# Block 0's rows written and asked for three units earlier, and three more x tiles made by ScalarE and GpSimd

## The chip, the cores and the metric

One core of one Trainium2 chip runs the whole kernel in a single launch. The metric is the device time of an execution in microseconds (us). TensorE is written PE here (PEld is its weight load), VectorE DVE, ScalarE ACT, GpSimd POOL, SyncE SP; SP issues nearly all DMA, POOL the indirect ones.

## The reference, cut to what matters

A decayed linear attention over 768 steps for 4 batches and 8 heads of 48, whose output rows (3072 of 384 numbers) go through a mixture of 8 experts, one expert for each row:

```python
for t in range(S):
    cur = np.einsum('bhd,bhe->bhde', u[None] * kt, vt)
    y[:, :, t] = np.einsum('bhd,bhde->bhe', rt, state + cur)
    state = wt[:, :, :, None] * state + np.einsum('bhd,bhe->bhde', kt, vt)
x = y.transpose(0, 2, 1, 3).reshape(B * S, H * D)
logits = x @ w_gate + modality_bias[modality_id]
e_idx = np.argmax(logits, axis=1)
for e in range(E):
    h = np.maximum(x[mask] @ w1[e], 0.0)
    out[mask] = gate_w[mask, None] * (h @ w2[e])
```

With the inputs drawn, 2663 rows go to expert 1 and 409 to expert 6. Of the rows of expert 1, the first five units of 128 rows hold 544 and the first ten 1110.

## The kernel before, in words

**Attention.** The 3072 rows are 24 units of 128 rows, six for each batch. A software pipeline runs `att_iter(i)` for i from -2 to 23. In iteration i it decays and scales the inputs of unit a = i + 2 (DVE makes the two scans B and E and then R; POOL makes K and G), multiplies keys with queries for unit m = i + 1 (PE; DVE masks the result to A; ACT carries the state) and makes the output of unit z = i on PE in the PSUM bank pY. One iteration later `x_rows(z - 1)` adds the term dV, which POOL makes, to pY and stores the row tile x (tile xp). It does so in one of two ways: DVE adds both in one instruction, or, for the iterations in `BY_TWO`, ACT copies pY to xp and POOL adds dV in place. One iteration after that, `x_cols` transposes x on PE and `logits` multiplies it with the gate.

PSUM is short: pK holds R's input of the next unit until DVE has made R, and PE's transposes of K into pK come after that; pY is written by the next unit's products only when x has read it.

**Routing.** At the end of iterations 11 and 12 two hooks route the first group of units (`CUT`: units 0 to 9): the row's expert, and by counting products on PE (`route_b`) the row's place `posT` in the DRAM table xs, which holds 3584 rows for each expert. A queue `pend` then holds the ten units; `drain(n)` takes n of them and lets POOL write their x rows to xs with an indirect DMA each (`scatter`). The other 14 units are routed and written while the experts run.

**Experts.** Rows are worked on in blocks of 512. Block 0 always takes the first 512 rows of expert e0, which is known from the biases alone. `blk_load(0)` reads them from xs with one DMA on SP's queue (tile xl) and one of the gate values (xg); `blk_t(0)` transposes xl on PE; then `blk_up` and `blk_down` run for each of eight slices of the hidden layer, each product three times with the weights split into a high part wh and a low part wl. The weights are split by ACT (wh) and POOL or DVE (wl), those of block 0 in iterations 22 and 23 (`w_splits`) and after. `table(0)` tells what block 1 is: it needs `hd`, which is 1 for e0 if block 0 was full.

**What sets the order.** Every engine has one queue in program order, written out by hand. `pend`, `hooks` and the sets `BY_TWO` and `SPLITS` set what goes into which iteration. SP waits at its head instruction, POOL too.

In the profile's lines, L241 is K, L306 G, L302 dV, L238 R, L347 A, L424 x by DVE, L421 and L422 x by ACT and POOL, L639 the scatter, L320 the transposes of K, L434 those of x, L272, L372, L384 and L387 further products of an iteration, L662 the load of xl, L687 its transposes, L709 and L731 the experts' products, L230 a half slice of wl.

Of the kernel before, what the change touches and what calls it, by code (L numbers as in the profile page):

```python
# [14 lines left out]
ALU = mybir.AluOpType  # L15
# [3 lines left out]
P = 128  # L19
NCH = S // P  # L20
NU = B * NCH
NT = B * S
DM = H * D
E, F = 8, 1024
# [5 lines left out]
BT = 512  # L30
# [20 lines left out]
NG = 8  # L51
CUT = (0, 10, NU)
NJS = (CUT[1], NU - CUT[1])
GW = B * H * S * D // (P * NG)
WHALF = FC // 2 * DM

# [2 lines left out]
def kernel(ctx: ExitStack, tc: tile.TileContext, rkw, vt, wf, cst, mid, wg, bias, w1, w2, out):  # L59
# [24 lines left out]
    T = {}  # L84

    def wt(n, tag, sh, bufs=None, dt=F32):
        T[tag, n] = (pa if tag in PREP else wk if tag in WORK else rt).tile(sh, dt, tag=tag, name=f"{tag}{n}", bufs=bufs)
        return T[tag, n]
# [68 lines left out]
    onesb = cp.tile([P, P], BF16, name="onesb")  # L157
# [13 lines left out]
    oh0 = cp.tile([P, E], F32, name="oh0")  # L171
# [68 lines left out]
    def mk_k(a, k):  # L240
        nc.gpsimd.tensor_tensor(out=wt(a, "K", [P, 4, P]), in0=quarters(k), in1=quarters(T["B", a][:, 1:517])[:, :, 1:129], op=ALU.mult)  # L241
# [23 lines left out]
    def ok(n):  # L265
        return 0 <= n < NU

    def delta(m, pT):
        G = T["G", m]
        for p in range(4):  # L270
            for q in (0, 64):
                nc.tensor.matmul(out=pT[q:q + 64, DM + 2 * p:DM + 2 * p + 2], lhsT=G[:, p * P + q:p * P + q + 64], rhs=ub[:, p, 0:2],  # L272
                                 start=True, stop=True, skip_group_check=True)
        nc.scalar.copy(out=wt(m, "dT", [P, 4, 2], 3), in_=pT[:, DM:DM + 8].rearrange("p (a b) -> p a b", a=4))

    st = quarters(pt("st", "pU")[:, 0:4 * D])
    hooks = []
    done = iter(range(2 * FC))

    SPLITS = {NU - 2: 4, NU - 1: 8}  # L280
    BY_TWO = (1, 4, 7, 8, 9, 10, 11)

    def w_splits(i):
        for _ in range(SPLITS.get(i, 0)):
# [2 lines left out]
    def att_iter(i):  # L287
        a, m, z = i + 2, i + 1, i
# [14 lines left out]
                                    in1=T["dT", z].rearrange("p a b -> p (a b)")[:, :, None].to_broadcast([P, H, D]), op=ALU.mult)  # L303
        if ok(a):
            mk_k(a, k)
            nc.gpsimd.tensor_tensor(out=wt(a, "G", [P, 512]), in0=r, in1=k, op=ALU.mult)  # L306
        if i == NU - 1:
            w_splits(i)
        if ok(z - 1):
            x_rows(z - 1, i in BY_TWO)  # L310
        last = first(m + 1)
        if ok(m):
            K, R, v = T["K", m], T["R", m], T["v", m]
# [36 lines left out]
            mk_r(a)  # L350
        if ok(m):
            delta(m, pT)
            if i < NU - 1:
                w_splits(i)
            if not last:
                for h in range(H):
                    p, hh = divmod(h, 2)

                    nc.tensor.matmul(out=st[64 * hh:64 * hh + rows, p], lhsT=KT[:, h],
                                     rhs=v[:, h * D:(h + 1) * D], start=first(m) and p == 0, stop=True, skip_group_check=True)  # L360
                carry(m)
# [92 lines left out]
    def rcol(o, *sh):  # L454
        n = 1
        for d in sh:
            n *= d
        v = T["R"][:, o:o + n]
        return v if len(sh) == 1 else v.rearrange("p (a b) -> p a b", a=sh[0])

    C_RK = NU * E
# [31 lines left out]
    def route_b(c):  # L493

        oh, nj = T["oh", c], NJS[c]
        sh, NE = [P, nj, E], nj * E
        pR = T["R"][:, C_RK:C_RK + NE + E]

        def add(out, lhsT, rhs, start=False, stop=False):
            nc.tensor.matmul(out=out, lhsT=lhsT, rhs=rhs, start=start, stop=stop, skip_group_check=True)  # L500

        add(pR[:, 0:NE], trib, oh.rearrange("p a b -> p (a b)"), c == 1)
        add(pR[:, 0:NE], onesb, ersb[:, None, :].to_broadcast(sh))
        if c:
            add(pR, onesb, ohs[:, None, :].to_broadcast([P, nj + 1, E]))

        for j in range(nj):
            add(pR[:, (j + 1) * E:], onesb, oh[:, j:j + 1].to_broadcast([P, nj - j, E]), stop=j == nj - 1)
        po, rk = posT[:, CUT[c]:CUT[c + 1]], rcol(C_RK, nj, E)
        nc.vector.tensor_tensor(out=rk, in0=rk, in1=oh, op=ALU.mult)  # L510
        with nc.allow_low_precision("whole numbers"):
            nc.vector.tensor_reduce(out=po, in_=rk, axis=AX.X, op=ALU.add)
# [3 lines left out]
    def table(ph):  # L516
# [51 lines left out]
        if ph == 0:  # L568
            rounded(g, ct, 1.0 / BT, -0.5 + 0.5 / BT)
            hd = wt(ph, "hd", [P, E], 1)  # L570
            tt(out=hd, in0=g, in1=oh0, op=ALU.min)
            tt(out=g, in0=g, in1=hd, op=ALU.subtract)
            sums(cu, g)
            yield

            ts(out=fs, in0=cu, scalar1=float(NA - 1), scalar2=None, op0=ALU.min)
            vec.scalar_tensor_tensor(out=fA, in0=cu[:, 1:E + 1], scalar=float(NA - 1), in1=fs[:, 0:E], op0=ALU.min, op1=ALU.subtract)
            yield from rows(1, NA - 1, cu, fA, hd)
            tt(out=fA, in0=fA, in1=hd, op=ALU.add)
            return  # L580
# [222 lines left out]
    pend = []  # L803
# [3 lines left out]
    def drain(n, after=None, h=None):  # L807
        for _ in range(n):
            if pend:
                if after:  # L810
                    after(h[0:1, 0:1].bitcast(F32))
                scatter(pend.pop(0))
# [11 lines left out]
    for i in range(-2, NU):  # L824
        if 2 <= i < 7:
            hooks.append((setup_a, setup_b, setup_c, setup_d, setup_e)[i - 2])
        if i == CUT[1] + 1:
            ra, tb = route_a(0), table(0)
            hooks.extend([lambda: list(ra), lambda: hook_b(0)])
        if i == CUT[1] + 2:  # L830
            route_x(0)
        if i >= NU - 2:
            hooks.append(lambda: next(tb))
        if i == NU - 1:
            prep.close()
        att_iter(i)
        if i == NU - 1:
            for n in done:
                w_split_half(n)
        if i != -1 and ok(i + 3):  # L840
            loadv(max(i + 3, 2))
        if ok(i + 6):
            load(i + 6, ((1024, 1541),))
        if i == 4:
            e0 = nc.sync.value_load(e0i[0:1, 0:1], min_val=0, max_val=E - 1)
        for n in range(2 * FC):
            if i == (n + 4 if n < FC // 2 else NU - 10 + n if n < FC else NU - 6 + (n - FC) // 2):
                w_raw(e0, n // FC, n % FC, parts=FC)
        if ok(i + 6):
            load(i + 6, ((0, 1024),))  # L850
        if i == -1:
            clear((ersb, 0.0), (onesb, 1.0), (one8, 1.0), (mfx, 0.0), (rbx, 0.0))
        if i == 0:
            clear((zt, 0.0), (zt[:, DM:DM + 1], 1.0), (zt[:, DM + 1:DM + 2].bitcast(I32), PAD_ID), (glo, W_LO), (ghi, -W_HI))
            early()
        if i == 4:
            r0 = nc.sync.value_load(e0r[0:1, 0:1], min_val=0, max_val=(E - 1) * RS)
        if 8 <= i < 8 + JT:
            rows_apart("xz", nc.sync.dma_start(out=xs[ds(r0 + (i - 8) * P, P), :], in_=zt))

        drain(1)
        if i == NU - 3:
            assert not pend
            blk_load(0)
    assert not pend and not hooks

# [302 lines left out]
```

## Time and profile before

| | |
|---|---|
| median of 3 runs | 336.15 us (335.85 to 338.52) |
| the profiled execution | 336.19 us, of it 334.4 us from the first to the last instruction |
| TensorE's granted clock | 0.996 of full speed over the span |
| busy shares of the span | PE 96%, PEld 88%, DVE 64%, ACT 61%, POOL 59% |
| instruction queues (kind "instruction") | 33 packets on q8, 25 on q14 |
| the chain that ended last | nearly empty: the last output write of POOL, 0.98 us |

Times within the span count from its first instruction. A row of the timeline gives the start, the duration, the engine, the line and in brackets how long the engine sat idle ahead of it and what ended that; "issue" stands where no other engine or DMA in the profile explains it. Ends of PE's products are modelled, so a long row of them overlaps the next row; their starts are the better measure.

### The profile page before, as it was taken

The page shows a single profiled execution, that of the slowest core. Times are in us where ns is not written, and L with a number is a line of the kernel's source. Part 1 is how long each engine was busy: PE and PEld are TensorE (multiplying, and loading weights), DVE is VectorE, ACT ScalarE, POOL GpSimd, SP SyncE. Part 2 cuts the span into 40 slices and gives each one's busy share as a digit, 9 for nine tenths or more (in the row PEclk, how much of TensorE's full clock was granted, in tenths as well). Part 3 has the DMA queues.
Part 4 walks back from the last instruction along what each step waited for, and adds up shares of the span by engine and source line. Part 5 has one row for each costly group of instructions (what it writes and reads, how often), then busy time and mean ns, then how long its engine had stood idle before and what let it go on. Part 6 is the DMA issues. An engine that isn't in the chain of part 4 may idle for free. (4 is left out here: it accounts for less than half of the span.)

```text
span 334.4 us, 10126 instructions
## 1 busy us (share of the span) xinstructions
PE 321.6 (96%) x3942; PEld 293.1 (88%) x3943; DVE 214.4 (64%) x376; ACT 204.2 (61%) x467; POOL 196.6 (59%) x226
## 2 busy tenths in 40 slices
PE   6899998999999999999999999999999999999993
PEld 3689898988899988899889988998899889999993
DVE  6999997999999757795333965934560464054230
ACT  3887897787488775542521767656745855632150
POOL 7988987879999795676361680247024603450041
PEclk9999999999999999999999999999999999999998
DMA  7997888878998532426337037026544763360011
GB/s 273 406 347 245 294 280 241 285 243 240 301 309 263 163 97 97 95 95 215 143 119 213 0 84 250 0 73 169 185 167 165 214 233 97 95 212 5 0 74 32
DMA packets 35586, 58.66 MB, mean 175 GB/s; under 512 B 17297, under 2 KB 22089, under 8 KB 35528
## 3 DMA queue, kind: packets, MB, share of 16 engines
q1 hardware_dynamic: 32424, 48.45, 46.4%
q0 software_dynamic: 3104, 9.47, 7.6%
q8 instruction: 33, 0.54, 0.7%
q14 instruction: 25, 0.20, 0.2%
HBM read 57.86 MB, written 12.67 MB: 211 GB/s over the span
## 5 line engine op out<-in xcount | busy, mean ns | idle before, releaser
L224 POOL TENSOR_TENSOR wl<-raw,wh 128x768 fp32r<-128x768 f32 x20 | 39.0, 1954 | 73.8 <-ACT wh L223 73.7
L223 ACT CAST wh<-raw 128x768 fp32r<-128x768 f32 x48 | 39.3, 831 | 37.4 <-PE pU_d L731 23.3
L720 DVE SCALAR_TENSOR_TENSOR h<-pS_u,h 128x512 fp32r<-128x512 f32 (+2 forms) x39 | 23.2, 607 | 36.5 <-ACT h L718 36.3
L751 POOL DMA_INDIRECT out<-ot,xg x24 | 25.2, 1052 | 29.4 <-ACT ot L760 23.4
L224 DVE TENSOR_TENSOR wl<-raw,wh 128x768 fp32r<-128x768 f32 x28 | 31.0, 1113 | 14.8 <-ACT wh L223 14.4
L709 PE MATMUL pS_u<-xh,wh 128*128 128x512 f32 (+1 forms) x102 | 39.6, 388 | 0.0
L709 PE MATMUL pS_u<-xh,wl 128*128 128x512 f32 (+1 forms) x102 | 39.2, 385 | 0.0
L709 PE MATMUL pS_u<-xo,wh 128*128 128x512 f32 (+1 forms) x102 | 39.2, 384 | 0.0
L718 ACT ACTIVATE h<-pS_u 128x512 fp32r<-128x512 f32 (+1 forms) x34 | 19.8, 586 | 27.7 <-PE pS_u L709 25.4
L731 PE MATMUL pX_d<-wh,h 128*128 128x384 f32 x96 | 32.4, 337 | 0.0
L731 PE MATMUL pY_d<-wh,h 128*128 128x384 f32 x96 | 32.2, 335 | 0.0
L731 PE MATMUL pK_d<-wh,h 128*128 128x384 f32 x96 | 32.1, 334 | 0.0
L639 POOL DMA_INDIRECT xs<-xp,posT x24 | 26.1, 1088 | 9.3 <-issue 7.4
L306 POOL TENSOR_TENSOR G<-in 128x512 f32<-128x512 f32 x24 | 30.7, 1278 | 0.0
L241 POOL TENSOR_TENSOR K<-in,B 128x512 f32<-128x512 f32 x24 | 28.4, 1185 | 3.7 <-PE pY L387 1.7
L295 DVE TENSOR_TENSOR_SCAN B<-in,pX_d 128x516 f32<-128x516 f32 x24 | 29.3, 1219 | 1.8 <-DMA in<-rkw 1.8
L298 DVE TENSOR_TENSOR_SCAN E<-in,pX_d 128x516 f32<-128x516 f32 x24 | 29.5, 1229 | 0.8
L731 PE MATMUL pU_d<-wh,h 128*128 128x384 f32 x80 | 26.8, 334 | 0.0
L720 DVE SCALAR_TENSOR_TENSOR h<-pT_u,h 128x512 fp32r<-128x512 f32 (+2 forms) x17 | 9.6, 577 | 24.6 <-ACT h L718 24.6
L387 PE MATMUL pY<-v,A 128*64 128x48 f32 x368 | 25.3, 222 | 0.0
L347 DVE TENSOR_TENSOR A<-pS,m 128x768 f32<-128x768 f32 x24 | 22.8, 948 | 3.7 <-PE pS L345 3.6
L387 PEld LDWEIGHTS pY<-v,A 128*64 128x64 f32 x368 | 23.8, 138 | 0.0
(239 smaller groups left out, 860.8 us busy)
## 6 DMA issues: line engine op xcount, KB each, us to landing
raw<-w SPq DMA_DIRECT2D x24, 768.0 KB
in<-rkw SPq DMA_DIRECT2D x23, 512.0 KB
v<-vt SPq DMA_DIRECT2D x24, 288.0 KB
in<-rkw SPq DMA_DIRECT2D x23, 258.5 KB
wg<-wf SPq DMA_DIRECT2D x8, 576.0 KB
xl<-xs SPq DMA_DIRECT2D x20, 192.0 KB
raw<-w SPq DMA_DIRECT2D x16, 192.0 KB
xs<-zt SPq DMA_DIRECT2D x12, 193.0 KB
```

What stands on the lines that cost most here:

```text
L223: nc.scalar.copy(out=wh[k][:, sl], in_=raw[k][:, sl])
L224: (eng or (nc.vector, nc.gpsimd)[k]).tensor_tensor(out=wl[k][:, sl], in0=raw[k][:, sl], in1=wh[k][:, sl].bitcast(F32), op=ALU.subtract)
L241: nc.gpsimd.tensor_tensor(out=wt(a, "K", [P, 4, P]), in0=quarters(k), in1=quarters(T["B", a][:, 1:517])[:, :, 1:129], op=ALU.mult)
L295: nc.vector.tensor_tensor_scan(out=Bt[:, 516:0:-1], data0=w[:, 516:0:-1], data1=d1[:, 516:0:-1], initial=0.0, op0=ALU.mult, op1=ALU.max)
L298: nc.vector.tensor_tensor_scan(out=Et, data0=w[:, 0:516], data1=d1[:, 1:2].to_broadcast([P, 516]), initial=1.0, op0=ALU.mult, op1=ALU.max)
L306: nc.gpsimd.tensor_tensor(out=wt(a, "G", [P, 512]), in0=r, in1=k, op=ALU.mult)
L387: nc.tensor.matmul(out=yh[64:P, g, sw, hh], lhsT=A[:, hh, g, 1 + sw], rhs=vs[:, g, hh] if sw else v[:, h * D:(h + 1) * D], start=new and n ...
L639: rows_apart("xs", nc.gpsimd.indirect_dma_start(out=xs[:, :], out_offset=bass.IndirectOffsetOnAxis(ap=posT[:, n:n + 1], axis=0), in_=T["xp ...
L709: nc.tensor.matmul(out=pp, lhsT=wsrc[0][:, f, c * P:(c + 1) * P], rhs=xsrc[:, c], start=(n == 0), stop=(n == 3 * KC - 1))
L720: nc.vector.scalar_tensor_tensor(out=h2[:, o:o + c1 - c0], in0=pp[:, c0:c1], scalar=0.0, in1=hh[:, c0:c1].bitcast(F32), op0=ALU.max, op1=A ...
L731: nc.tensor.matmul(out=X["y", q][j], lhsT=hsrc[:, j * P:(j + 1) * P], rhs=wsrc[1][:, f], start=(f == 0 and n == 0), stop=(last and n == 2))
L751: ins = nc.gpsimd.indirect_dma_start(out=out[:, :], out_offset=bass.IndirectOffsetOnAxis(ap=xg[0:n, j, 1:2].bitcast(I32), axis=0), in_=ot[ ...
```

## The change

`route_b(0)` counts one column group more after the first `N0` = 5 units, and `hd` is 1 where this count for e0 has reached 512, so block 0 now stands for the first five units alone. The ten scatters stood at the ends of iterations 12 to 21; now five stand at the ends of 13 to 17, two at the ends of 20 and 21, and three within iteration 22, ahead of its weight splits. `blk_load(0)` moves from the end of iteration 21 to the end of 18. Iterations 12, 18 and 19 make x by ACT and POOL instead of DVE, and in these and in iteration 4 the x step stands between K and G on POOL (`X_FIRST`) instead of behind G.

```diff
@@ -51,6 +51,7 @@
 NG = 8
 CUT = (0, 10, NU)
 NJS = (CUT[1], NU - CUT[1])
+N0 = 5
 GW = B * H * S * D // (P * NG)
 WHALF = FC // 2 * DM
 
@@ -276,9 +277,11 @@
     st = quarters(pt("st", "pU")[:, 0:4 * D])
     hooks = []
     done = iter(range(2 * FC))
+    S0 = 13
 
     SPLITS = {NU - 2: 4, NU - 1: 8}
-    BY_TWO = (1, 4, 7, 8, 9, 10, 11)
+    BY_TWO = (1, 4, 7, 8, 9, 10, 11, 12, 18, 19)
+    X_FIRST = (4, 12, 18, 19)
 
     def w_splits(i):
         for _ in range(SPLITS.get(i, 0)):
@@ -303,10 +306,12 @@
                                     in1=T["dT", z].rearrange("p a b -> p (a b)")[:, :, None].to_broadcast([P, H, D]), op=ALU.mult)
         if ok(a):
             mk_k(a, k)
+            if i in X_FIRST:
+                x_rows(z - 1, True)
             nc.gpsimd.tensor_tensor(out=wt(a, "G", [P, 512]), in0=r, in1=k, op=ALU.mult)
         if i == NU - 1:
             w_splits(i)
-        if ok(z - 1):
+        if ok(z - 1) and i not in X_FIRST:
             x_rows(z - 1, i in BY_TWO)
         last = first(m + 1)
         if ok(m):
@@ -350,6 +355,8 @@
             mk_r(a)
         if ok(m):
             delta(m, pT)
+            if i == NU - 2:
+                drain(CUT[1] - N0 - 2)
             if i < NU - 1:
                 w_splits(i)
             if not last:
@@ -505,7 +512,8 @@
             add(pR, onesb, ohs[:, None, :].to_broadcast([P, nj + 1, E]))
 
         for j in range(nj):
-            add(pR[:, (j + 1) * E:], onesb, oh[:, j:j + 1].to_broadcast([P, nj - j, E]), stop=j == nj - 1)
+            more = int(c == 0 and j < N0)
+            add(T["R"][:, C_RK + (j + 1) * E:C_RK + (nj + 1 + more) * E], onesb, oh[:, j:j + 1].to_broadcast([P, nj - j + more, E]), stop=j == nj - 1)
         po, rk = posT[:, CUT[c]:CUT[c + 1]], rcol(C_RK, nj, E)
         nc.vector.tensor_tensor(out=rk, in0=rk, in1=oh, op=ALU.mult)
         with nc.allow_low_precision("whole numbers"):
@@ -568,7 +576,7 @@
         if ph == 0:
             rounded(g, ct, 1.0 / BT, -0.5 + 0.5 / BT)
             hd = wt(ph, "hd", [P, E], 1)
-            tt(out=hd, in0=g, in1=oh0, op=ALU.min)
+            vec.scalar_tensor_tensor(out=hd, in0=rcol(C_RK + (NJS[0] + 1) * E, E), scalar=float(BT), in1=oh0, op0=ALU.is_ge, op1=ALU.mult)
             tt(out=g, in0=g, in1=hd, op=ALU.subtract)
             sums(cu, g)
             yield
@@ -858,9 +866,9 @@
         if 8 <= i < 8 + JT:
             rows_apart("xz", nc.sync.dma_start(out=xs[ds(r0 + (i - 8) * P, P), :], in_=zt))
 
-        drain(1)
-        if i == NU - 3:
-            assert not pend
+        if S0 <= i < S0 + N0 or NU - 4 <= i < NU - 2:
+            drain(1)
+        if i == S0 + N0:
             blk_load(0)
     assert not pend and not hooks
 
```

POOL in iteration 12, before. A number behind a name is the unit (K14 is K of unit 14, dV13 of unit 13); xp0 and xp1 are the x tiles of the first ten and of the other units.

```order
L302 TENSOR_TENSOR dV12_1537<-v12_1319,dT12_1470 128x384
L241 TENSOR_TENSOR K14_1539<-in2_91,B14_1532 128x512
L306 TENSOR_TENSOR G14_1541<-in2_91 128x512
L639 DMA xs_65<-xp0_381,posT_154 29184x386
L302 TENSOR_TENSOR dV13_1651<-v13_1405,dT13_1590 128x384
```

The same place on POOL after the change.

```order
L305 TENSOR_TENSOR dV12_1537<-v12_1319,dT12_1470 128x384
L242 TENSOR_TENSOR K14_1539<-in2_91,B14_1532 128x512
L429 TENSOR_TENSOR xp1_1421<-xp1_1421,dV11_1415 128x384
L311 TENSOR_TENSOR G14_1543<-in2_91 128x512
L305 TENSOR_TENSOR dV13_1649<-v13_1405,dT13_1591 128x384
```

The scatter has left this iteration, and the addition for x of unit 11 stands ahead of G14; iterations 18 and 19 look like this too, and in iteration 4 the addition and G6 have changed places.

SP's queue at the end of iteration 21, before, where tab is the table of the later blocks and the ISA rows are steps on SP's registers.

```order
L218 DMA raw1_68<-w2 128x384
L659 TENSOR_LOAD e0r_160
L659 ISA x2
L662 ISA
L662 DMA xl0_2591<-xs_65 128x4x384
L666 ISA
L666 DMA xg0_2592<-xs_65 128x4x2
L650 TENSOR_LOAD tab_165
```

SP's queue at the end of iteration 18 and the start of 19, after.

```order
L219 DMA raw1_68<-w2 128x384
L667 TENSOR_LOAD e0r_160
L667 ISA x2
L670 ISA
L670 DMA xl0_2262<-xs_65 128x4x384
L674 ISA
L674 DMA xg0_2263<-xs_65 128x4x2
L100 DMA v22_2377<-vt 128x576
```

The load of block 0 now has the values of units 22 and 23 (v22, v23) and nine weight loads behind it on SP, where only the table's registers stood.

POOL from the end of iteration 21 to 23, before.

```order
L306 TENSOR_TENSOR G23_2493<-in3_92 128x512
L639 DMA xs_65<-xp0_381,posT_154 29184x386
L302 TENSOR_TENSOR dV22_2604<-v22_2367,dT22_2542 128x384
L230 TENSOR_TENSOR wl0_70<-raw0_67,wh0_69 128x192 x4
L302 TENSOR_TENSOR dV23_2694<-v23_2476,dT23_2642 128x384
L230 TENSOR_TENSOR wl0_70<-raw0_67,wh0_69 128x192 x12
```

The same place after.

```order
L311 TENSOR_TENSOR G23_2500<-in3_92 128x512
L647 DMA xs_65<-xp0_381,posT_154 29184x386
L305 TENSOR_TENSOR dV22_2598<-v22_2377,dT22_2549 128x384
L647 DMA xs_65<-xp0_381,posT_154 29184x386 x3
L231 TENSOR_TENSOR wl0_70<-raw0_67,wh0_69 128x192 x4
L305 TENSOR_TENSOR dV23_2697<-v23_2483,dT23_2636 128x384
L231 TENSOR_TENSOR wl0_70<-raw0_67,wh0_69 128x192 x12
```

Three scatters stand ahead of block 0's first four half slices of wl and of dV23.

## Rows read from the trace of the kernel before

**Rows 1.** Waits of PE from 16 to 60 and 60 to 120 us; total, times, longest.

```profile
PE pY L384 <- issue: 1.1, 1, 1.1
...
PE pT L272 <- issue: 0.2, 1, 0.2
...
PE pT L272 <- issue: 1.0, 1, 1.0
```

**Rows 2.** Timeline of PE: first up product of blocks 0, 1 and 2.

```profile
123.70 0.50 PE L709 MATMUL pS_u<-xh,wh 128*128 128x512 f32 x1
...
158.26 0.39 PE L709 MATMUL pT_u<-xh,wh 128*128 128x512 f32 x1
...
191.29 0.39 PE L709 MATMUL pS_u<-xh,wh 128*128 128x512 f32 x1
```

**Rows 3.** Timeline of PE and of POOL, iterations 4 and 5.

```profile
33.27 0.66 PE L320 MATMUL pK<-cs,K 128*128 128x128 f32 x4
34.20 0.55 PE L434 MATMUL pT<-cs,xp 128*128 128x128 f32 x3 [0.28 <-POOL xp L422]
...
35.51 0.63 PE L272 MATMUL pT<-cs,G 128*64 128x2 f32 x16
...
31.91 1.28 POOL L306 TENSOR_TENSOR G<-in 128x512 f32<-128x512 f32 x1
33.13 1.01 POOL L422 TENSOR_TENSOR xp<-xp,dV 128x384 f32<-128x384 f32 x1
```

**Rows 4.** Timeline of PE, iteration 13.

```profile
71.51 0.63 PE L320 MATMUL pK<-cs,K 128*128 128x128 f32 x4 [0.16 <-DVE R L238]
71.98 0.49 PE L434 MATMUL pT<-cs,xp 128*128 128x128 f32 x3
...
73.22 0.63 PE L272 MATMUL pT<-cs,G 128*64 128x2 f32 x16
...
74.92 0.88 PE L372 MATMUL pY<-SPb,R 128*64 128x96 f32 x16 [0.34 <-DVE xp L424]
```

**Rows 5.** Timeline of DVE, iterations 12 and 13.

```profile
69.38 0.53 DVE L424 TENSOR_TENSOR xp<-pY,dV 128x384 f32<-128x384 f32 x1
69.82 0.95 DVE L347 TENSOR_TENSOR A<-pS,m 128x768 f32<-128x768 f32 x1
...
74.33 0.53 DVE L424 TENSOR_TENSOR xp<-pY,dV 128x384 f32<-128x384 f32 x1
```

**Rows 6.** Timeline of POOL: G of iteration 12, the first and the last scatter.

```profile
70.58 1.27 POOL L306 TENSOR_TENSOR G<-in 128x512 f32<-128x512 f32 x1
72.75 1.18 POOL L639 DMA_INDIRECT xs<-xp,posT  x1 [0.90 <-POOL G L306]
...
112.62 1.01 POOL L639 DMA_INDIRECT xs<-xp,posT  x1 [0.17 <-issue]
```

**Rows 7.** Timeline of SP and of PE: block 0's load, its transposes, unit 23's x.

```profile
116.88 0.39 SPq L662 DMA_DIRECT2D xl<-xs  x1
...
120.44 0.55 PE L434 MATMUL pT_('x', 0)_2740<-cs,xp 128*128 128x128 f32 x3
121.35 0.72 PE L687 MATMUL pX_x<-cs,xl 128*128 128x128 f32 x4 [0.36 <-DMA xl<-xs]
...
122.83 0.49 PE L434 MATMUL pT_('x', 1)_2773<-cs,xp 128*128 128x128 f32 x3
```

**Rows 8.** Timeline of POOL, iterations 22 and 23.

```profile
116.75 2.26 POOL L230 TENSOR_TENSOR wl<-raw,wh 128x192 fp32r<-128x192 f32 x4 [2.25 <-ACT wh L229]
118.96 0.83 POOL L302 TENSOR_TENSOR dV<-v,dT 128x384 f32<-128x384 f32 x1
```

**Rows 9.** Busy time of PE, PEld, DVE, ACT, POOL; then PE clock, DMA share, GB/s.

```profile
80.00:84.00 4.00, 3.31 (x78) 2.94 (x74) 3.93 (x7) 3.26 (x10) 3.80 (x5) 1.00 0.94 263
...
100.00:105.00 5.00, 5.00 (x129) 4.63 (x127) 4.93 (x7) 4.69 (x15) 4.79 (x6) 1.00 0.92 292
...
117.00:121.00 4.00, 3.99 (x84) 3.56 (x82) 1.98 (x7) 2.93 (x11) 4.00 (x8) 1.00 0.72 202
```

## The prediction

> **What bounds the kernel now.** Read the table first: PE is busy 96% of the span at full clock. Then its waits: between 16 and 160 us there are seven. Three are called "issue", 1.1, 0.2 and 1.0 us [rows 1]; the other four are the brackets of PE's rows in the timeline, 0.28 for x by POOL, 0.16 for R by DVE, 0.34 for x by DVE, 0.36 for the load of xl [rows 3, 4, 7], 3.4 us in all. Everywhere else one product follows the next. So DVE and POOL, busy as they are, cost the time only what these brackets say, and the end moves by what becomes of the seven, and by any new one.
>
> From 123.70 us on PE runs the experts. One block takes 191.29 - 158.26 = 33.0 us [rows 2], the change leaves the number of blocks as it is, and PE does not wait there in the time that the waits cover. I therefore take what follows the first up product as a fixed length, and ask only how much earlier that product starts. All times below are on the clock of the trace before; the sum is made against its own 336.19 us, which is within 0.1 us of the median of 336.15.
>
> **The change part by part.**
>
> *Iteration 4, x ahead of G.* POOL makes G from 31.91 and then x from 33.13 to 34.14; PE is through K's transposes and stands until 34.20 [rows 3]. In iteration 13, where nothing held it, the same step followed 71.98 - 71.51 = 0.47 after K's transposes [rows 4]; here that would be 33.74, so the loss is 34.20 - 33.74 = 0.46. With the two steps exchanged x starts at 31.91, ends at 32.92, and the loss goes. G6 then ends 32.92 + 1.28 = 34.20, and PE wants it at 35.51 - 0.46 = 35.05 [rows 3]: hidden with 0.85 to spare. What is late next is nothing that I see. **Gain 0.46**; its lower end is the 0.28 that the row counts as idle.
>
> *Iteration 12, x by two engines, no scatter.* DVE's x of unit 11 holds back its next instruction by 69.82 - 69.38 = 0.44 [rows 5]. The two waits behind it are both DVE's: PE waits 0.16 for R at 71.51 and 0.34 for the x that ends 74.33 + 0.53 = 74.86, and goes on at 74.92 [rows 4, 5]. Without the first wait PE would be ready at 74.92 - 0.34 - 0.16 = 74.42; DVE, 0.44 earlier, lets it go at 74.48. **Gain 0.44**. On ACT a copy of the tile is new; the nearest row is DVE's x, 0.53. It costs between nothing, if ACT has a gap there, and 0.53, if R's input comes that much later and R with it, which would eat the gain. I take nothing: ACT is busy 61% of the span, and the wait for R ends with DVE's own work, which never sits idle for ACT's in these rows.
>
> On POOL the addition (1.01 as in [rows 3]) takes the place of the scatter, which cost 72.75 + 1.18 - 70.58 - 1.27 = 2.08 with the wait in front [rows 6]. It starts where G started, at 70.58, and ends at 71.59; PE's x step wants it at 71.98 - 0.16 = 71.82 [rows 4]. G14 ends 71.59 + 1.27 = 72.86; PE wants it at 73.22 - 0.16 = 73.06. Both fit with only 0.2 to spare, the narrowest place of the change. If POOL is 0.4 late here, half of this gain goes.
>
> *Block 0's load.* SP sends it at 116.88, since its ten scatters must have landed, the last of which starts at 112.62 [rows 6, 7]: 4.26 later. PE waits 0.36 for it at 121.35. The scatters are ten at about equal steps from 72.75 to 112.62, one each 4.43 us; iteration 17's is the sixth and stands near 94.9. So SP sends the load near 94.9 + 4.3 = 99.2, and with the 121.35 - 116.88 = 4.5 that it took to arrive it is there by 104, 17 us ahead of need. **Gain 0.36**. Its upper end is 121.35 less 120.44 and the 0.42 or so that three transposes take before the next can start, 0.49. What is late next: the transposes need only xl; what follows them on PE is unit 23's x at 122.83 [rows 7].
>
> *The queues that the load is moved past.* On SP the values of units 22 and 23 and nine weight loads now stand behind it. They are held until about 99.2, and their buffers come free at about that pace anyway; the weights are split from 116 on [rows 8]. Priced at nothing; the cover is some 10 us. On POOL the scatter of iteration 20 now has to wait until the load has read xs, near 104; it stands near 108. Nothing again.
>
> *Three scatters in iteration 22.* POOL sat idle 2.25 us ahead of the half slices of wl there [rows 8]. Three scatters at 1.01 to 1.18 with 0.17 in front of each are 3.5 to 4.1 us [rows 6]. So wl and dV23 come 1.3 to 1.8 later: dV23 ends at 118.96 + 0.83 + 1.8 = 121.6 at the worst, and with DVE's 0.53 for x of unit 23 that is 122.1. POOL itself is earlier by the first two gains, 0.90, which leaves 121.2; PE wants this x at 122.83 less all three, 121.57 [rows 5, 7, 8]. Hidden by 0.4 at the worst and 0.9 at the best, so priced at nothing; without that cover it would cost what is missing, tenths.
>
> *Iterations 18 and 19* take 0.44 from DVE each; none of the seven waits lies there: nothing. The extra counting columns and the other instruction for hd are as long as those they replace.
>
> **Sum.** 0.46 + 0.44 + 0.36 = 1.26; 336.19 - 1.26 = 334.93, so **334.9 us**, 0.4% below before. Between the ends (0.28 + 0 + 0.36 = 0.64, and 0.46 + 0.50 + 0.49 = 1.45) it is 334.7 to 335.6.
>
> **A wait that no row explains.** The two long "issue" waits, 1.1 and 1.0 us, are ended by no engine and no DMA of the program [rows 1]. The second lies in a stretch where PE is busy 3.31 of 4 us and the DMA engines 0.94 [rows 9], and the core's instructions come by DMA too, 33 packets on one queue. I read them as PE out of instructions because a packet came late. The load moves 0.79 MB from a stretch at 0.72 into one at 0.92 [rows 9]. The Trainium skill (Runtime: NRT & Kernel Launch, Instruction fetch mechanics) says that the next block of instructions is fetched while the current one runs and that the cost of crossing into it is mostly hidden. The trace does not show it hidden in this place; by that rule alone a busier stretch would cost nothing here and the sum would stay at 334.9. The Trainium skill (DMA: Bandwidth & Descriptors, Issuing engines are not separate DMA queues) says that transfers of all issuers run on the same 16 engines and interleave, which speaks against moving a load into a busy stretch.
>
> **The rivals.**
>
> *Slower: late instructions between 96 and 110 us.* Mechanism: block 0's rows share the DMA engines with the weight and value loads, at 0.92 already, and an instruction packet comes late. Each time costs PE 1.0 to 1.1 [rows 1]. One such wait gives 334.9 + 1.1 = 336.0, two give 337.1, slower than before: it decides from the second on. For it: the two waits that exist. Against it: PE has none in that stretch now although it is as busy as where they lie, and two scatters leave iterations 18 and 19.
>
> *A wait of this kind goes.* What runs from iteration 5 on shifts by some tenths against the DMA traffic, and a scatter of 0.2 MB goes at 72.75. One fewer: 333.9; both: 332.8.
>
> *A gain is hidden anyway.* If POOL misses the 0.2 us in iteration 13, if ACT's copy delays R, or if unit 23's x is late, one gain of the three is lost: 334.93 + 0.44 = 335.4.
>
> *It does not do what it says.* If the first five units held fewer than 512 rows of e0, block 0's rows would be taken again by another block: 334.9 + 33.0 = 368. The inputs hold 544 of them, so this needs other inputs.
>
> **How the numbers follow.** Forecast as summed 0.52; one wait more 0.16, two more 0.04; one wait fewer 0.14, both gone 0.04; a gain lost 0.08; another block 0.01, and 0.01 for what I do not see. The range from 333.6 to 336.4 holds the forecast, the lost gain, one wait more and one fewer, 0.90 together, and leaves out 0.10; as the ends of the terms are half a us wide I make it no narrower. A change by 1%, 3.4 us, is about the least that a measurement of this kernel can tell from none. Faster than 332.8 needs both waits gone and a little more: 0.04. Slower than 339.5 needs another block or something unseen: 0.02. Within 1%: 0.94.
>
> **What would show each step right or wrong.** Right: in the waits of PE those for x by POOL, for R and x by DVE and for xl are gone or under 0.1 us; block 0's load goes out near 99 us on SP; the first up product stands near 122.4 instead of 123.70; and the distance from it to the end is unchanged. Wrong: PE waits for G or x of POOL in iteration 13, or for x at unit 23's transposes; POOL's scatter of iteration 20 waits for the load; "issue" waits of about 1 us stand in another number than two.

## The result and the profile after

The changed kernel takes **339.77 us** (median of 6 runs, 337.22 to 340.62), the kernel before 335.62 beside it (6 runs): a ratio of **1.0102, 95% interval 1.0056 to 1.0148**. It is slower by 1.0%, where 0.4% faster was forecast, and lies outside the range. The profiled execution took 339.63, with a span of 337.8. Executions over 1.5% above the fastest of their kernel count in the medians below and not in the ratios, so a ratio can differ from that of its medians.

The three gains came. PE's waits of after, 16 to 60 and 60 to 120 us (total, times, longest), against [rows 1]:

```profile
PE pY L394 <- issue: 0.6, 1, 0.6
...
PE pT L273 <- issue: 0.8, 2, 0.4
PE pT L273 <- ACT xT L442: 0.7, 2, 0.4
PE pS L350 <- issue: 0.5, 2, 0.3
```

No row for x by POOL, R, x by DVE or xl is left in the timeline either. New is a wait for ACT (0.37 and 0.32): PE's products of L273 write into the bank pT, out of which ACT first has to copy the transposed x. PE where it takes up the x made in iteration 4, then in iteration 13, against [rows 3, 4]:

```profile
33.13 0.66 PE L325 MATMUL pK<-cs,K 128*128 128x128 f32 x4
33.62 0.49 PE L441 MATMUL pT<-cs,xp 128*128 128x128 f32 x3
...
70.20 0.66 PE L325 MATMUL pK<-cs,K 128*128 128x128 f32 x4
70.69 0.49 PE L441 MATMUL pT<-cs,xp 128*128 128x128 f32 x3
```

From K's transposes to x's it is now 0.49 in both places. In the first it was 0.93; in iteration 13 this step was free before too, and the gain there is that the two waits for DVE are gone from the list above. SP, then PE, at block 0's load, at the first up product and at that of block 1, against [rows 2, 7]:

```profile
98.19 0.39 SPq L670 DMA_DIRECT2D xl<-xs  x1
...
123.37 0.55 PE L441 MATMUL pT_('x', 0)_2743<-cs,xp 128*128 128x128 f32 x3
...
126.00 0.50 PE L717 MATMUL pS_u<-xh,wh 128*128 128x512 f32 x1
...
160.57 0.39 PE L717 MATMUL pT_u<-xh,wh 128*128 128x512 f32 x1
```

The load goes out at 98.19 instead of 116.88. From x's transposes of unit 22 to the first up product it takes 126.00 - 123.37 = 2.63 instead of 3.26. But that product starts at 126.00, 2.30 later than before; from there on everything on PE is shifted by 2.31 until the last down product, as assumed. (The last outputs land another 1.0 later; a second profile of the kernel before ends that way too.)

So the loss that the change explains lies ahead of 126 us. At 98 us the changed kernel is 1.78 ahead (K's transposes of iteration 19 start at 98.33 instead of 100.11). PE in iteration 22:

```profile
113.57 0.55 PE L441 MATMUL pT<-cs,xp 128*128 128x128 f32 x3
114.05 1.17 PE L350 MATMUL pS<-R,K 64*64 64x128 f32 x29
115.55 0.34 PE L350 MATMUL pS<-R,K 64*64 64x64 f32 x3 [0.34 <-issue]
116.21 0.37 PE L273 MATMUL pT<-cs,G 128*64 128x2 f32 x6 [0.32 <-ACT xT L442]
116.99 0.47 PE L273 MATMUL pT<-cs,G 128*64 128x2 f32 x10 [0.42 <-issue]
117.28 1.42 PE L379 MATMUL pY<-SPb,R 128*64 128x96 f32 x16
...
119.17 0.90 PE L441 MATMUL pK<-cs,xp 128*128 128x128 f32 x3
```

From x's transposes here to those of iteration 23 (the first and the last row) it takes 5.60; before it was 116.99 - 114.10 = 2.89. PE stands three times, twice ended by nothing that the trace shows, and then the products themselves are slow. POOL, ACT and DVE in the same iteration, against [rows 6, 8]:

```profile
114.07 0.97 POOL L647 DMA_INDIRECT xs<-xp,posT  x1 [0.30 <-issue]
115.34 0.97 POOL L647 DMA_INDIRECT xs<-xp,posT  x1 [0.30 <-issue]
118.16 2.24 POOL L231 TENSOR_TENSOR wl<-raw,wh 128x192 fp32r<-128x192 f32 x4 [1.85 <-ACT wh L230]
...
115.58 0.48 ACT L442 COPY xT<-pT 128x384 f32<-128x384 f32 x1 [1.57 <-PE pT L441]
...
117.22 0.96 DVE L352 TENSOR_TENSOR A<-pS,m 128x768 f32<-128x768 f32 x1 [1.76 <-PE pS L350]
```

ACT waits 1.57 and DVE 1.76 for products of PE that the rows above have as ended at 114.12 and 115.89. An engine learns that another's product is done by a semaphore; here these came 1.45 and 1.31 after the modelled ends, and below I call that a late report of PE. POOL is not late by its own work; wl waits for ACT. Busy time in stretches of 1 us (PE, PEld, DVE, ACT, POOL, then PE's granted clock, DMA share, GB/s):

```profile
115.00:116.00 1.00, 0.55 (x9) 0.29 (x4) 0.47 (x1) 0.42 (x2) 0.69 (x2) 1.00 0.41 156
116.00:117.00 1.00, 0.38 (x7) 0.35 (x7) 0.00 (x0) 0.66 (x3) 0.31 (x1) 1.00 0.31 114
117.00:118.00 1.00, 1.00 (x21) 1.00 (x22) 0.78 (x1) 0.44 (x3) 0.00 (x0) 0.75 0.36 133
118.00:119.00 1.00, 1.00 (x21) 1.00 (x17) 0.18 (x1) 0.84 (x4) 0.84 (x2) 0.50 0.00 0
...
121.00:122.00 1.00, 1.00 (x31) 1.00 (x28) 0.36 (x1) 1.00 (x5) 1.00 (x3) 1.00 0.09 16
```

PE falls to 0.55 and 0.38, and after that the granted clock is 0.50, the level of 1.2 GHz, until 121; the 16 products of L379 take 1.42 (0.88 for the same products, there L372, in [rows 4]). The stops fall between 114.5 and 117.0; three scatters run in a row on POOL from 112.8 to 116.3.

### The profile page after: what moved, and what is told of

It reads as the page before. It is cut to its first block, busy times and chain, and to the rows that moved or that the text cites. A ratio compares the mean times of both kernels' runs of the same rounds, so it can differ in the third digit from the quotient of the medians.

```text
span 337.8 us, 10127 instructions
## 1 busy us (share of the span) xinstructions
PE 325.0 (96%) x3943; PEld 295.2 (87%) x3943; DVE 213.0 (63%) x373; ACT 205.1 (61%) x470; POOL 199.1 (59%) x229
```

## The experiments

- Theory A: the three scatters in a row stop PE.
- Theory B: block 0's load, moved into a busy stretch, makes PE's instructions late. Theory D: it does so only together with x made by two engines in 18 and 19.
- Theory C: the copies of x on ACT in 18 and 19 cost the time.
- Later, theory E: the loss falls on some executions by chance; theory F: it belongs to the program.

Four chips took part (A to D; that of the first measurement isn't recorded); runs of one job share a chip and are compared with the kernel before in that job. "Step 22" is the time from x's transposes in iteration 22 to those in 23, in the profiled execution.

| kernel | chip | median, us | before there | ratio, 95% interval | step 22 |
|---|---|---|---|---|---|
| changed, first | ? | 339.77 | 335.62 | 1.0102 (1.0056-1.0148) | 5.60 |
| changed, 2nd: e5 | A | 335.24 | 334.86 | 1.0006 (0.9976-1.0035) | 2.89 |
| changed, 3rd: f1 | B | 341.41 | 336.65 | 1.0102 (1.0051-1.0152) | 5.01 |
| changed, 4th: g1 | C | 338.50 | 335.86 | 1.0070 (1.0033-1.0107) | 4.80 |
| three scatters later: e1 | A | 341.49 | 335.48 | 1.0196 (1.0145-1.0247) | 2.88 |
| three multiplications: e3 | A | 342.59 | 335.48 | 1.0210 (1.0168-1.0252) | 2.88 |
| the same: h4 | D | 344.97 | 335.30 | 1.0265 (1.0187-1.0343) | 2.88 |
| x of 18, 19 by DVE: e2 | A | 336.55 | 335.48 | 1.0034 (0.9999-1.0069) | 2.89 |
| the same: g2 | C | 339.02 | 335.86 | 1.0075 (1.0035-1.0115) | 4.48 |
| scatters apart: g3 | C | 336.73 | 335.86 | 1.0022 (0.9985-1.0058) | 3.50 |
| apart, 18, 19 by DVE: f3 | B | 338.31 | 336.65 | 1.0015 (0.9967-1.0063) | 2.88 |
| early load alone: e7 | A | 335.31 | 334.86 | 1.0004 (0.9983-1.0025) | 2.88 |
| before, three in 20: e4 | A | 335.34 | 335.48 | 0.9987 (0.9962-1.0011) | 2.88 |
| the same: h3 | D | 337.45 | 335.30 | 1.0050 (1.0022-1.0078) | 2.88 |
| before, 18, 19 by two: e6 | A | 339.52 | 334.86 | 1.0114 (1.0068-1.0161) | 2.89 |
| before, 4 and 12: e8 | A | 336.80 | 334.86 | 1.0036 (1.0007-1.0064) | 2.88 |
| 4, 12, three in 20: h1 | D | 341.20 | 335.30 | 1.0160 (1.0116-1.0204) | 2.88 |
| 4, three in 20: h2 | D | 337.97 | 335.30 | 1.0052 (1.0024-1.0080) | 2.88 |
| before again: f2 | B | 335.91 | 336.65 | 0.9980 (0.9948-1.0013) | 2.88 |

**The three scatters out of iteration 22 (e1, e3, h4).** Both edits move them behind iteration 23; the second puts POOL work of 2.64 us in the place of their 3.55:

```diff
             if i == NU - 2:
-                drain(CUT[1] - N0 - 2)
+                for _ in range(3):                 # e3 and h4 alone
+                    nc.gpsimd.tensor_tensor(out=zt[:, 0:DM], in0=zt[:, 0:DM], in1=zt[:, 0:DM], op=ALU.mult)
...
             blk_load(0)
+    drain(CUT[1] - N0 - 2)
     assert not pend and not hooks
```

> The changed kernel with the three scatters of iteration 22 moved behind iteration 23, where block 1's load, 30 us ahead of its use, is all that waits for them. Theory A (the three scatters back to back hold up what PE reports to DVE and ACT, and the half clock follows from the idle PE): iteration 22 takes 2.9 us again instead of 5.60 between its two transposes of x, no stretch at 1.2 GHz near 118 us, time 339.8 - 2.7 = 337.1. Theory B (instructions for PE arrive late because block 0's load moved into a busy stretch): iteration 22 stays near 5.6, time 339.8. Theory C (x by two engines in iterations 18 and 19 makes ACT the late engine): iterations 19 to 21 still lose 1.2 us, and iteration 22 is not told apart by this run.

> As the first of these kernels, with three multiplications of a 128x384 tile of zeros on POOL in the place where the three scatters stood, 1.01 us each as x by POOL is. Theory A in its first form (it is the scatter as such, its descriptors and its small packets): iteration 22 takes 2.9 us, time 337.1. Theory A in its second form (it is the 3.5 us of POOL ahead of block 0's half slices of wl and of dV23): iteration 22 takes about 5 us, time near 339.8.

> The changed kernel with three multiplications on POOL in place of the three scatters of iteration 22, which stand behind iteration 23, a second time, for its profile between 113 and 118 us. If it is POOL's time that stops PE there: late reports of PE and 4 us or more in iteration 22. If it is the scatters: 2.9 us, whatever the chip, and pauses, if any, at the scatters of iterations 20 and 21. Its loss of 4 to 6 us behind 125 us is its own and stays (the second weight's halves take the place of the rows that the late scatters read).

Step 22 takes 2.88 in all three, but the times are worse. That is the edit's own price, which I had not foreseen for e1 and e3: ACT's row, then PE's, of e1.

```profile
130.90 0.83 ACT L224 CAST wh<-raw 128x768 fp32r<-128x768 f32 x1 [6.27 <-DMA xs<-xp,posT]
...
133.01 0.80 PE L715 MATMUL pS_u<-xh,wh 128*128 128x512 f32 x1 [4.50 <-DVE h L726]
```

ACT's copy of the second weight may write its place only when the late scatters have read x of the first ten units from it; h is late, PE waits 4.5, and the slow clock follows (the first up product starts at 121.60, 2.1 earlier than before, and all from 143 us on stands 4.08 later). So the times say nothing on theory A, and step 22 on chip A says nothing either, as e5 will show. Chip D tells: in h4 the lone scatters of iterations 20 and 21 make PE report 1.12 and 0.84 late, and the multiplications do nothing. POOL, then PE:

```profile
112.76 2.64 POOL L360 TENSOR_TENSOR zt<-zt 128x384 f32<-128x384 f32 x3
...
113.77 0.55 PE L442 MATMUL pT<-cs,xp 128*128 128x128 f32 x3
...
116.65 0.55 PE L442 MATMUL pK<-cs,xp 128*128 128x128 f32 x3
```

**x of 18 and 19 by DVE (e2, g2).**

```diff
-    BY_TWO = (1, 4, 7, 8, 9, 10, 11, 12, 18, 19)
-    X_FIRST = (4, 12, 18, 19)
+    BY_TWO = (1, 4, 7, 8, 9, 10, 11, 12)
+    X_FIRST = (4, 12)
```

> The changed kernel with x of units 17 and 18 by DVE, as in the kernel before; all else as changed. Theory C (the copy on ACT in iterations 18 and 19 makes PE wait for xT): the waits of 0.37 and 0.32 us for ACT go, iteration 19 no longer loses its 0.4 and iterations 20 and 21 perhaps not their 0.9; time 338.5 to 339.4, and if the clock's fall depends on them, 336.7. Theory A (scatters): iteration 22 still takes 5.6 us; time 339.4 to 339.8.

> The changed kernel with x of 18 and 19 by DVE, the three scatters of iteration 22 left as they are, on the same chip as the changed kernel. If the three scatters make the loss of iteration 22 by themselves, it stands here when it stands in the changed kernel. If it takes x by two engines in 18 and 19 as well (ACT later against PE), iteration 22 takes 2.9 us here in any case, and the time is 3 to 4 us under that of the changed kernel.

e2 seemed to settle it for theory C: 3.2 us less than the changed kernel. It did not; the two had run on different chips. Beside the changed kernel on chip C, g2 is no faster (339.02 against 338.50) and loses 1.6 in step 22 as well. What theory C is worth is 0.39, below.

**The kernel before with its last three scatters in a row (e4, h3).**

```diff
+            if i == NU - 4:
+                drain(3)
             if i < NU - 1:
                 w_splits(i)
...
-        drain(1)
+        if i < NU - 5:
+            drain(1)
```

> The kernel before, whose scatters of iterations 19, 20 and 21 stand back to back in iteration 20, between delta and the state; block 0's load stays behind iteration 21, x as before. Theory A, first form: PE loses 1 to 2.7 us in iterations 20 and 21 through late reports to DVE and ACT, time 337 to 338.5. Theory A, second form, or B or C: POOL makes K and G of the next units 2.5 us later, which PE would show as waits for POOL of up to that size and nothing else; with B or C alone and POOL's slack enough, 335.6.

> The kernel before with the scatters of 19, 20 and 21 in a row in iteration 20, a second time. On the chip where it ran first (0.9987 of before) no scatter stopped PE, the three of the changed kernel neither. If the chip of this job stops PE at scatters, reports of PE stand 0.7 to 1.5 us late behind the second and third of them, near 107 to 111 us, and the time is 1 to 3 us over before; if not, 335.

On chip A nothing happens, on chip D the kernel before gets 0.5% slower by this alone. The profiled execution of h3 took 340.17, 2.7 over its median, so its rows show more than the median lost. The last two of POOL's three scatters, PE, ACT, and busy time and clock in stretches of 2 us:

```profile
108.10 0.98 POOL L641 DMA_INDIRECT xs<-xp,posT  x1 [0.30 <-issue]
109.38 0.98 POOL L641 DMA_INDIRECT xs<-xp,posT  x1 [0.30 <-issue]
...
109.85 0.95 PE L320 MATMUL pK<-cs,K 128*128 128x128 f32 x4
111.01 0.80 PE L436 MATMUL pT<-cs,xp 128*128 128x128 f32 x3 [0.21 <-issue]
...
111.34 0.48 ACT L323 COPY KT<-pK 128x384 f32<-128x384 f32 x1 [2.76 <-PE pK L320]
...
108.00:110.00 2.00, 1.19 (x15) 0.81 (x11) 1.93 (x3) 0.57 (x2) 1.60 (x2) 1.00 0.99 265
110.00:112.00 2.00, 1.69 (x11) 1.06 (x14) 0.64 (x2) 0.64 (x2) 2.00 (x3) 0.76 0.96 332
112.00:114.00 2.00, 2.00 (x48) 1.88 (x44) 0.62 (x1) 1.44 (x4) 1.58 (x2) 0.50 0.26 99
```

PE ended K's transposes at 110.80 by its row, ACT hears of it at 111.32 and had waited 2.76; PE is busy 1.19 of 2 us; then the clock is at 1.2 GHz. In e4 the same stretch is busy 2.00 of 2 at full clock. On chip D the stops stand at the scatters in iteration 20; they need neither iteration 22 nor the early load of block 0.

**The changed kernel again (e5, f1, g1), and the kernel before (f2).** No edit.

> The changed kernel once more, unchanged, for a second profile and more times. If the 5.6 us of iteration 22 and the half clock behind it are a property of the kernel, both stand here again, within some tenths, and the time is 339.8 again. If they belong to the one execution that was profiled, iteration 22 takes 2.9 us here, the time is still 339.8 as its runs said, and the loss stands in another place.

> The changed kernel a third time. Theory E (the loss of 4 us that was measured first is PE's late instructions and a half clock behind them, which fall in some executions and not in others, and its own terms come to -1.2): iteration 22 takes 2.9 us in the profile unless an issue wait stands in it, the waits of iterations 4, 12 and for xl are gone, PE waits 0.4 for ACT's xT; time between 334 and 338. Theory F (the changed kernel is slower by itself and the second measurement was the exception): 339 to 340.5 and the 5.6 us of iteration 22 again.

> The changed kernel a fourth time, beside the two variants of this job. Two of three measurements gave 1.010 times the time before, with 5.0 to 5.6 us for iteration 22 and a half clock behind it; one, on another chip, 1.001 without either. Either is expected here: 339 to 341 with the loss in iteration 22, or 335 without.

> The kernel before once more, as a kernel of its own, for a second profile. Theory E: its two issue waits of 1.3 and 1.2 us are not both here, in the same places; the waits for x by POOL in iteration 4, for R and x by DVE in 13 and for xl are here, since they belong to the program; time 334.5 to 336.

e5: PE in iteration 22, then the second of the three scatters, then ACT.

```profile
113.08 0.55 PE L441 MATMUL pT<-cs,xp 128*128 128x128 f32 x3
...
114.39 0.63 PE L273 MATMUL pT<-cs,G 128*64 128x2 f32 x16
114.88 0.86 PE L379 MATMUL pY<-SPb,R 128*64 128x96 f32 x16
...
115.97 0.55 PE L441 MATMUL pK<-cs,xp 128*128 128x128 f32 x3
...
114.32 0.97 POOL L647 DMA_INDIRECT xs<-xp,posT  x1 [0.30 <-issue]
...
113.67 0.48 ACT L442 COPY xT<-pT 128x384 f32<-128x384 f32 x1 [0.47 <-PE pT L441]
```

The same program with the same scatters, and ACT takes up x 0.04 after PE's transposes end. Nor is it a matter of where the scatters fall against PE: in e2, also on chip A, x's transposes start 0.91 after the first of the three (0.81 in the first measurement), and step 22 takes 2.89. On B and C it is as in the first measurement: two scatters in, PE reports x 1.45 and 1.42 late, stands in pieces of 0.2 to 0.5, and the clock falls. g1, PE, then ACT:

```profile
114.14 0.55 PE L441 MATMUL pT<-cs,xp 128*128 128x128 f32 x3
...
118.94 0.55 PE L441 MATMUL pK<-cs,xp 128*128 128x128 f32 x3
...
116.13 0.48 ACT L442 COPY xT<-pT 128x384 f32<-128x384 f32 x1 [1.97 <-PE pT L441]
```

Theories E and F were both half right: the loss stands in this program in three of its four measurements, and is absent in the one on chip A. f2 is the miss that matters most. All its waits of PE, 16 to 60 and 60 to 125 us:

```profile
PE pT L272 <- issue: 0.5, 1, 0.5
...
PE pT L272 <- issue: 1.2, 1, 1.2
PE pS L345 <- issue: 0.4, 1, 0.4
```

I expected the waits for x by POOL, for R and x by DVE and for xl to be here, since the program is the same. None is. PE waits 2.1 us in all instead of 3.4, in other places and to issue alone, and what it would have waited for is ready when it comes. Its first up product starts at 122.88, 0.82 earlier than in the first profile; the span is 334.4 again because the last outputs land later. Its last scatter, too, makes PE report 1.04 late.

**Scatters apart (g3, f3), and the early load alone (e7).** In g3 one scatter moves ahead of the load and one to the end of iteration 22; f3 adds the edit of e2; e7 has scatters in 12 to 18 and x as before.

```diff
             if i == NU - 2:
-                drain(CUT[1] - N0 - 2)
+                drain(1)                           # not in e7
...
-        if S0 <= i < S0 + N0 or NU - 4 <= i < NU - 2:
+        if S0 <= i <= S0 + N0 or NU - 4 <= i < NU - 1:    # e7: i <= S0 + N0 or ...
```

> The changed kernel with x of 18 and 19 by two engines, but the scatters apart: one more ahead of block 0's load in 18, one in iteration 22 in its old place and one at its end. If the three scatters in a row make the loss, iteration 22 takes 2.9 us here and the time is 3 to 4 us under that of the changed kernel where that has the loss. If x of 18 and 19 makes it, the loss is here too.

> The changed kernel without its parts that cost: x of 18 and 19 by DVE, one scatter more before block 0's load (13 to 18), then one each in 20 and 21 and two in 22, apart. Its own terms by the profiles so far: -0.49 (iteration 4), -0.48 (iteration 12), -0.63 (xl), 1.6 less than before, 333.3; by the prediction's terms 1.26 less, 333.6. If issue waits come more often with the early load: no gain, 335.

> Block 0's load alone is moved: scatters in 12 to 18, the load at the end of 18, scatters in 20, 21 and 22; x by the engines of the kernel before. As predicted: the wait of 0.36 for xl goes, 335.1. If the load's traffic makes PE's instructions late between 100 and 112 us (theory D): one or two waits of 0.6 to 0.8 more there, 336 to 337. If block 0's load and x in 18 and 19 cost only together: 335.1.

g3, POOL's scatter of iteration 22, then PE:

```profile
114.29 1.01 POOL L647 DMA_INDIRECT xs<-xp,posT  x1 [0.17 <-issue]
...
113.19 0.55 PE L441 MATMUL pT<-cs,xp 128*128 128x128 f32 x3
...
114.98 0.28 PE L379 MATMUL pY<-SPb,R 128*64 128x96 f32 x1
115.57 0.80 PE L379 MATMUL pY<-SPb,R 128*64 128x96 f32 x14 [0.31 <-issue]
...
116.69 0.55 PE L441 MATMUL pK<-cs,xp 128*128 128x128 f32 x3
```

One scatter, one stop of 0.31, step 22 of 3.50 against 4.80 on the same chip, and full clock: the median is 1.8 under the changed kernel's, though the intervals of the two ratios overlap. In f3 step 22 is free, but two waits at the ends of instruction blocks (last section), at 108.76 and 115.00, take 2.2 in the iterations ahead. e7 shows that the early load by itself brings PE no issue wait over 0.2 between 96 and 117 us on chip A. None of the three is under the kernel before.

**Parts alone (e6, e8, h1, h2).**

```diff
+    X_FIRST = (18, 19)       # e6; (4, 12) in e8 and h1; (4,) in h2
...
-        drain(1)
+        if i < NU - 6 or i == NU - 3:      # e6; 12 < i < NU - 5 or i == NU - 3 in e8;
+            drain(1)                       # 12 < i < NU - 4 in h1; i < NU - 5 in h2; drain(3) in 20 in all
```

> The kernel before with x of units 17 and 18 by ACT and POOL, ahead of G, and nothing else of the change; the scatters of iterations 18 and 19 stand with that of 20, which cost nothing where it was tried. Block 0's load stays late. Theory C (x by two engines in 18 and 19 is what costs): 2 to 3 us slower than before, 337.5 to 338.5, with waits of PE for ACT's xT from iteration 19 on. Theory D (it costs only together with block 0's load at 98 us, whose traffic makes PE's instructions late): within 0.5 of before, 335 to 336.

> The two gains in the attention alone: x ahead of G by two engines in iterations 4 and 12, no scatter in 12 (three in 20, the others in 13 to 18 and 21), block 0's load late, x of 18 and 19 by DVE. As predicted for these two steps: 0.46 + 0.44 below before, 334.6. If they are hidden behind other waits: 335.5.

> The kernel before with the attention's two gains and block 0's load left late but its last scatter earlier: x ahead of G by two engines in 4 and 12, scatters in 13 to 19 and three in 20, the load behind iteration 21. By the profiles so far: -0.49 (iteration 4), -0.48 (iteration 12), -0.6 (the rows land sooner, the wait for xl goes as in the kernel with three scatters in 20): 1.6 under before. If scatters late in the attention stop PE on this chip, each of the three takes 0.4 to 1 us back and the time is that of before.

> The same without the part in iteration 12: x ahead of G in 4 alone, scatters in 12 to 18 and three in 20. 0.49 + 0.6 = 1.1 under before, or that of before if the three scatters stop PE.

e6 and e8 don't tell what they were meant to. Both leave the last scatter and block 0's load at the end of iteration 21, as the kernel before does, and PE comes to it 0.5 earlier. In e6 the load goes out at 116.68 (116.88 in [rows 7]), but its rows are there 0.9 later; why they take longer, no run shows. PE in e6:

```profile
122.24 0.72 PE L692 MATMUL pX_x<-cs,xl 128*128 128x128 f32 x4 [1.75 <-DMA xl<-xs]
```

That is 1.75 where [rows 7] had 0.36; in e8's profiled execution, which took 340.04, a slow clock follows. The median of e6, 339.52, holds a loss that its profiled execution, 336.90, doesn't show. What can be read is 0.39 more in iteration 19 and no other loss between 96 and 119 us in e6: theory C at its real size. h1 and h2 were to be under both kernels. On chip D the three scatters in 20 cost PE 4.0 and 2.2 between 105 and 114 us (against the same steps of e4), and h1 has a wait of 1.71 at the end of an instruction block with the slow clock behind it. No version here beats the kernel before.

## Why the prediction was wrong

**Iteration 4**: priced 0.46, measured 0.44 to 0.49. **Iteration 12**: priced 0.44; from iteration 12's K transposes to 14's it is 0.46 less. **Block 0's load**: priced 0.36, measured 0.63 (3.26 to 2.63), above its upper end of 0.49; the load went out at 98.19 (99.2 forecast), and the queues behind it kept nobody waiting. The length from the first up product to the last down product did not change. Against the profile that I had, 1.58 were gained where 1.26 was forecast. But the waits do not stand in every execution; they are there when PE is early and gone when an instruction block came late ahead of them. Iteration 4's is whole in four of the six profiles without its edit (0.2 in h3, none in f2), iteration 13's in four of seven (none in e4 and f2), that for xl in one of the two profiles of the kernel before. By these shares, as an estimate, 0.3 of each is left, and with ACT's 0.39 a gain of 0.5; on chip A, where no profile shows a stop at a scatter, e5 is 0.2 over before with an interval of -0.8 to +1.2, which holds it and can't tell it from nothing. I had priced a wait of one profile as if it stood in all.

**Iterations 18 and 19** were priced at nothing, since no wait of PE lay there. ACT's copies of x make it the late engine: PE waits for xT once, and iteration 19 takes 0.38 to 0.45 more in eight of the nine profiles that have them.

**The step that failed is "Three scatters in iteration 22".** It asked only when POOL would come to wl and dV23, and there it was right: PE never waits for x of unit 23, and three multiplications in their place cost PE nothing in step 22. It put what a scatter does to PE itself at nothing, without a reason. In the first measurement the two lone scatters of iterations 20 and 21 cost 0.38 and 0.47 and the three in a row 1.91 by standing (113.57 to 117.28 takes 3.71, in e5 1.80) and 1.55 by the slow clock behind it (to the next 128x96 products of L379: 3.86, in e5 2.31). The sum by these sizes, with 0.39 for ACT: -1.58 + 0.39 + 0.85 + 3.46 = 3.1 slower against the profile before. It shows 2.30: at 98 us the changed kernel is 1.78 ahead and not 0.95, mainly because its waits at the ends of instruction blocks (last section) are shorter, and that is luck of these two executions. The medians are 4.15 apart. Of that 2.3 stand here and 1.0 in the last outputs; the rest is mainly that the profiled execution before took 0.6 more than its median, which the waits that come and go may explain.

**The rivals.** Late instructions between 96 and 110 us did not make the first measurement's loss: its pauses there stand at scatters, not at block ends. But the mechanism is not refuted. Measured against the same places in the other profiles, PE loses 0.7 to 1.9 us at two block ends between 105 and 116 us in five of the twelve profiles with the early load (e2, e3, f3, g1, g2), and nothing there in the eight with the late one; so few can't decide whether the load does it. None of the rivals let an operation of POOL stop PE, and the chances left 0.01 for what was not seen. "A wait of this kind goes" has something to it: the step with the wait at 83.11 is 0.7 to 1.4 over its shortest in all seven profiles with a scatter in iteration 12, and 0 to 0.8 in twelve of the thirteen others.

**What stays open.** Why scatters stop PE on some chips and not on A, and whether it is the chip at all: A ran two jobs without a stop, each other chip one job with stops. Why three in a row cost more than three times one, and what makes an instruction block late. How often the three waits stand is known from two to seven profiles only.

## What to carry to other kernels

An indirect scatter can cost more than its second on POOL: look whether PE's reports get late around it, and before several are moved together into a stretch in which PE has no slack, try them apart. Price a short wait from two profiles: one that is gone in the second can give back less on the median than it shows. And compare two kernels only within one job: theory C lived on a difference of 1% between two chips.

## What the runs showed of the hardware

**Scatters and PE.** In the 20 profiles, PE's reports to ACT or DVE ahead of 122 us are late by 0.6 us or more 21 times; each time a scatter is running or ended within 1.3 us, in 7 of the 12 profiles that are not known to be of chip A and in none of the 8 that are. PE's issue waits say the same. Of 94 between 16 us and the first up product, 74 end at instruction blocks (below); the other 20 all stand at a scatter, by the same measure, in 8 of those 12 profiles. A scatter alone is not enough: all 21 late reports and 18 of the 20 waits lie behind 105 us, and the scatters ahead of that, five to eight in each of the 12 profiles, give but two waits, of 0.15 and 0.19. What is different behind 105 us, no run shows. A lone scatter lets PE go on before its rows move: in the changed kernel the scatter of iteration 21 ends on POOL at 111.72, PE starts nothing from 111.67 to 112.01, and the scatter's packets run from 112.29 to 113.02. The Trainium skill (Perfetto Trace Analysis, DMA Instruction — SWDGE (GPSIMD)) says that the row of such a DMA ends when its descriptors are generated, not when the data have moved; the trace agrees. So PE's stop at this scatter falls into the end of the making of its descriptors or just behind it. What joins the two, no run shows.

**Instruction blocks.** Counting PE's weight loads, products and semaphore instructions from the start, those 74 issue waits end at numbers that are 193 to 195 above a multiple of 256; the stops at the three scatters of iteration 22 lie at 5423 to 5449, where the nearest such numbers are 5313 and 5569. The page of the kernel before has an instruction queue with 33 packets of 16,384 bytes, and PE's 7,885 weight loads and products are about 31 times 256; so I take it for PE's. The Trainium skill (Runtime: NRT & Kernel Launch, Instruction fetch mechanics) names blocks of 16 KiB or 256 instructions, which agrees. The same section of the Trainium skill calls the cost of crossing into a block mostly hidden. By number the traces agree, as two to seven of the 21 crossings in this stretch show in an execution, but where one shows, PE waits 0.16 to 1.71 us.

**The clock.** Stretches at a granted clock of 0.50, each of about 3.4 or 6.8 us, stand behind waits of PE: behind the three scatters in the first measurement (117.5 to 120.9), f1 and g1, and behind those of iteration 20 in h1 and h3; in e8 behind 1.64 for xl, in h1 also behind 1.71 at a block end, in e1 behind 4.5 for h. In e6 (1.75 for xl) and in g2 and h2 (scatters, PE busy 1.03 and 1.10 of 2 us) it stayed at 1.00. What decides between the two, these rows don't show.
